# V as the moving operand in four column tiles, and shared weight loads for the scores, in a decode attention and MLP kernel

## The chip, the cores and the metric

The kernel runs on one core of a Trainium2 chip (trn2). The time is microseconds on the device. Before the change it is 372.0 us, the median of three runs (371.48 to 372.11).

## The reference

One token for each of 8 sequences goes through a gated mix of two branches: attention over a window of 2,048 cached positions, and an MLP.

```python
W = min(4096, max(256, Sk // 4))              # 2048
q = (x @ wq)                                  # 8 x 32 heads x 128
k = k_cache[:, :, Sk - W:, :]                 # 8 x 16 KV heads x 2048 x 128, bf16
v = v_cache[:, :, Sk - W:, :]                 # the same size; two query heads share a KV head
p = softmax(q k^T * Dh**-0.5)
a = (p v) @ wo                                # wo: 4096 x 576
b = gelu(layernorm(x) @ w1 + b1) @ w2 + b2    # w1: 576 x 4608, w2: 4608 x 576
out = g * a + (1 - g) * b                     # g = sigmoid(x . gate_w)
```

K and V of the window are 134 MB, the weights about 20 MB, and every byte is used for few rows only: one of K or V for the two query heads that share it, one of a weight for the 8 tokens. The kernel is a stream of loads.

## The kernel before

The sync engine issues one long list of loads. K and V come in "units" of 2 MB (four sequences of one head); 32 units each, in nine SBUF slots of 16 KB per partition. A group is four K units (all sequences of two heads). A planner orders every engine's work from estimated costs. The w2 chunks come last.

For a K unit, VectorE transposes K in place, then TensorE multiplies it by block-diagonal queries. Each 512-column matmul has its own weight load, although four in a row use the same one:

```python
for ee in range(2):
    for rc in range(4):
        rhs = bass.AP(arena, offset=aoffs("KT") + kb * 4096 + rc * 1024 + ee, ap=[[AST, 128], [2, 512]])
        mm = e.matmul(ps[:, rc, :], qbd[:, ub, 2 * h + ee, :], rhs, start=False, stop=(q == 3 and h == 1 and ee == 1))
```

For a V unit, V itself is the stationary operand, in 64 loads of 128x128, and eight probability columns move over each:

```python
for r in range(64):
    mm = e.matmul(ps[:, BK_OS[item % 2], 8 * (q % 2):8 * (q % 2) + 8], slot(s)[:, r * 128:(r + 1) * 128],
                  PT[:, g % 2, r, 8 * q:8 * q + 8],
                  start=(q % 2 == 0 and r == 0), stop=(r == 63), skip_group_check=True)
```

## Time and profile before

| what | before | where it is read |
|---|---|---|
| device time, median of 3 | 372.0 us | times |
| span of the profiled run | 369.5 us | page, first line |
| data queue, share of 16 engines' span | 98.5% | page, part 3 |
| TensorE, weight loads, VectorE, ScalarE busy | 65, 37, 57, 8% | page, part 1 |
| TensorE clock in the last four slices | 0.5 to 0.6 | page, part 2 |

In the profiles PE is TensorE's matmuls, PEld its weight loads, DVE VectorE, ACT ScalarE, POOL GpSimd and SP the sync engine; `ps` is PSUM, the memory that matmuls write, and `arena` the kernel's SBUF. These are the rows of the page's second part that matter (the span in 40 slices: granted TensorE clock in tenths, DMA busy in tenths, GB/s) and, from the third, the data queue and the queue of the instructions (packets, MB, share of 16 engines):

```profile
PEclk9999998799698879686898879696957788785556
DMA  8999999999999999999999999999999999999994
GB/s 343 426 422 424 427 432 431 434 424 431 429 431 429 413 436 427 429 427 429 435 426 429 414 431 432 431 431 426 426 435 433 418 424 427 435 429 426 413 420 167
...
q1 hardware_dynamic: 14848, 154.29, 98.5%
q8 instruction: 24, 0.39, 0.4%
```

DMA is at 9 tenths in every slice but the ends, and the data queue at 98.5%, so the loads bound the kernel. The instructions themselves are also read by DMA: the page has a queue of them, with 24 packets of 16 KB.

The groups of instructions by line (busy us, mean ns, then the idle time before them) for the weight loads of the scores and the products with V:

```profile
L641 PEld LDWEIGHTS ps<-arena 128*128 128x128 bf16 x512 | 52.5, 109 | 129.2 <-DVE arena L627 53.2 <-issue 39.2
L663 PE MATMUL ps<-arena 128*128 128x8 bf16 x2048 | 56.4, 166 | 12.3 <-DMA arena<-in_A_v_cache_dram 12.3
```

The timeline of TensorE at the end of the kernel before (start us, us, line, count, and the idle time before with what ended it):

```profile
357.10 2.33 PE L530 MATMUL ps<-arena 128*8 128x288 bf16 x18 [0.51 <-DMA arena<-in_B_w_dram]
360.06 2.33 PE L530 MATMUL ps<-arena 128*8 128x288 bf16 x18 [0.63 <-DMA arena<-in_B_w_dram]
363.15 3.96 PE L530 MATMUL ps<-arena 128*8 128x288 bf16 x36 [0.77 <-DMA arena<-in_B_w_dram]
...
367.25 0.45 DVE L734 CAST arena<-ps 8x288 bf16<-8x288 f32 x1 [14.28 <-PE ps L530]
```

The first three lines are w2 chunks 0, 1, and 2 with 3.

What the DMA engines do is in the windows view (start and end, length; busy us and counts of PE, PEld, DVE, ACT and POOL; then clock, DMA share and GB/s).

### The profile page before, as it was taken

What the parts mean: (1) busy time and instruction counts of PE and PEld (TensorE: products, weight loads), DVE (VectorE), ACT (ScalarE), POOL (GpSimd) and SP (SyncE); (2) the same over time, 40 slices, a digit from 0 to 9 for tenths busy, and PEclk for the clock granted to TensorE, in tenths of its full rate; (3) what the DMA queues carried; (4) which work ended last, traced back from release to release, by engine and by line L of the source; (5) the groups of instructions that cost most, each with busy time, mean ns of one, the idle gap of its engine ahead of it and who ended that gap; (6) DMA issues with size and microseconds to landing.
All of it is one profiled execution on the core that took longest, in us unless ns stands there. A gap on an engine that the chain in (4) does not pass through costs nothing.

```text
span 369.5 us, 7044 instructions
## 1 busy us (share of the span) xinstructions
PE 242.0 (65%) x3089; PEld 137.5 (37%) x3117; DVE 210.0 (57%) x253; ACT 28.6 (8%) x85; POOL 37.5 (10%) x163
## 2 busy tenths in 40 slices
PE   0349983896695486663965395755767385783376
PEld 0339430454242243232523243432424243343343
DVE  0704699688694663459744764478544964464000
ACT  1010001100300200003000300003000300003000
POOL 7030010011011001000101010100101000000000
PEclk9999998799698879686898879696957788785556
DMA  8999999999999999999999999999999999999994
GB/s 343 426 422 424 427 432 431 434 424 431 429 431 429 413 436 427 429 427 429 435 426 429 414 431 432 431 431 426 426 435 433 418 424 427 435 429 426 413 420 167
DMA packets 14934, 154.77 MB, mean 419 GB/s; under 512 B 1292, under 2 KB 5428, under 8 KB 6072
## 3 DMA queue, kind: packets, MB, share of 16 engines
q1 hardware_dynamic: 14848, 154.29, 98.5%
q8 instruction: 24, 0.39, 0.4%
q14 instruction: 6, 0.05, 0.0%
q10 hardware_dynamic: 56, 0.03, 0.0%
HBM read 154.31 MB, written 0.01 MB: 418 GB/s over the span
## 4 chain that ended last, share of the span: by engine, by line
DMA 63%; PE 20%; DVE 13%; SPq 2%; issue 1%; DVEq 0%
DMA arena<-in_A_k_cache_dram 42%; PE ps L641 12%; DMA arena<-in_B_w_dram 11%; DMA arena<-in_A_v_cache_dram 10%; DVE arena L627 9%; PE ps L663 3%; DVE arena L574 2%; PE ps L487 2%; SPq L716 1%; PE ps L530 1%; PE ps L637 1%; SPq L657 1%; PE ps L489 1%; DVE arena L577 0%; DVE arena L593 0%
## 5 line engine op out<-in xcount | busy, mean ns | idle before, releaser
L627 DVE STREAM_TRANSPOSE arena<-arena 128x2048 f32<-128x2048 f32 x64 | 145.0, 2296 | 79.1 <-DMA arena<-in_A_k_cache_dram 74.6
L641 PE MATMUL ps<-arena 128*128 128x512 bf16 x491 | 144.6, 449 | 45.1 <-DVE arena L627 44.0
L641 PEld LDWEIGHTS ps<-arena 128*128 128x128 bf16 x512 | 52.5, 109 | 129.2 <-DVE arena L627 53.2
L663 PE MATMUL ps<-arena 128*128 128x8 bf16 x2048 | 56.4, 166 | 12.3 <-DMA arena<-in_A_v_cache_dram 12.3
L663 PEld LDWEIGHTS ps<-arena 128*128 128x128 bf16 x2048 | 56.1, 97 | 19.1 <-DMA arena<-in_A_v_cache_dram 14.2
L620 POOL COPY arena<-arena 32x32 bf16<-32x32 bf16 x128 | 26.0, 203 | 177.2 <-PE ps L641 162.6
L637 PE MATMUL ps<-arena 128*128 128x512 bf16 x25 | 12.3, 630 | 40.2 <-DVE arena L593 36.7
L588 ACT ACTIVATE arena<-ps,arena 128x512 bf16<-128x512 f32 x32 | 21.5, 685 | 107.4 <-DVE arena L583 107.4
L574 DVE TENSOR_REDUCE arena<-ps 128x1 f32<-128x2048 f32 x8 | 18.3, 2282 | 17.7 <-PE ps L641 17.7
L593 DVE STREAM_TRANSPOSE arena<-arena 128x512 bf16<-128x512 bf16 x32 | 19.9, 675 | 0.9 <-ACT arena L588 0.9
L637 PEld LDWEIGHTS ps<-arena 128*128 128x128 bf16 x32 | 3.5, 128 | 42.9 <-DVE arena L593 38.5
L530 PE MATMUL ps<-arena 128*8 128x288 bf16 (+1 forms) x140 | 14.7, 377 | 3.1 <-DMA arena<-in_B_w_dram 1.9
L685 POOL TENSOR_TENSOR arena<-arena 128x16 bf16<-128x16 f32 x15 | 4.0, 265 | 121.2 <-ACT arena L678 121.2
L678 ACT ACTIVATE arena<-ps 128x16 f32<-128x16 f32 x15 | 2.8, 184 | 170.2 <-PE ps L663 170.2
L487 PE MATMUL ps<-arena 128*128 128x8 bf16 x144 | 10.9, 201 | 4.6 <-DMA arena<-in_B_w_dram 4.6
L487 PEld LDWEIGHTS ps<-arena 128*128 128x128 bf16 x144 | 10.8, 160 | 5.0 <-DMA arena<-in_B_w_dram 5.0
L530 PEld LDWEIGHTS ps<-arena 128*8 128x8 bf16 (+1 forms) x140 | 7.1, 106 | 10.9 <-DMA arena<-in_B_w_dram 3.6
L599 DVE RECIPROCAL arena<-ps 128x32 f32<-128x32 f32 x8 | 2.9, 358 | 11.4 <-PE ps L598 11.4
L409 PE MATMUL ps<-arena 8*128 8x8 bf16 x8 | 0.5, 167 | 13.4 <-DVE arena L382 9.7
L734 DVE CAST arena<-ps 8x288 bf16<-8x288 f32 x1 | 0.4, 446 | 14.3 <-PE ps L530 14.3
L685 DVE TENSOR_TENSOR arena<-ps,arena 128x16 bf16<-128x16 f32 x1 | 0.2, 228 | 14.0 <-PE ps L663 14.0
L489 PE MATMUL ps<-arena 128*128 128x8 bf16 x36 | 7.2, 201 | 0.0
(79 smaller groups left out, 79.4 us busy)
## 6 DMA issues: line engine op xcount, KB each, us to landing
arena<-in_A_k_cache_dram SPq DMA_DIRECT2D x32, 2048.0 KB, 34.0
arena<-in_A_v_cache_dram SPq DMA_DIRECT2D x32, 2048.0 KB, 34.4
arena<-in_B_w_dram SPq DMA_DIRECT2D x1, 4608.0 KB, 24.2
arena<-in_A_wo_dram SPq DMA_DIRECT2D x4, 1152.0 KB, 37.3
arena<-in_A_wq_dram SPq DMA_DIRECT2D x1, 4096.0 KB, 13.0
arena<-in_B_w_dram SPq DMA_DIRECT2D x3, 1296.0 KB, 14.8
arena<-in_B_w_dram SPq DMA_DIRECT2D x2, 576.0 KB, 20.5
arena<-in_A_wq_dram SPq DMA_DIRECT2D x1, 512.0 KB, 3.6
```

Source lines behind the costliest of these rows:

```text
L487: ins = e.matmul(out_, lhsT, yT[:, kt, :], start=(kt == 0), stop=False)
L489: ins = e.matmul(out_, lhsT, yT[:, 4 + c // 2, :], start=False, stop=True)
L530: ins = e.matmul(ps[32 * j:32 * j + 8, BK_ACC, 0:JN], lhsT, rhs[:, JN * j:JN * j + JN], start=False, stop=True, skip_group_check=True, til ...
L574: mx = add("dve", lambda e: e.tensor_reduce(out=k(MX), in_=ps[:, 0:4, :].rearrange("p a n -> p (a n)"), axis=AXL.X, op=ALU.max), deps=[qk_ ...
L588: return e.activation(out=Pm[:, 512 * c:512 * c + 512], in_=ps[:, c, :], func=ACTF.Exp, bias=k(NB), scale=SCALE, accum_out=k(SUM + c))
L593: pts.append(add("dve", (lambda c=c: lambda e: e.transpose(PT[:, g % 2, 16 * c:16 * c + 16, :].rearrange("p r m -> p (r m)"), Pm[:, 512 * ...
L620: return e.tensor_copy(dst, src)
L627: tr = add("dve", (lambda h=h, kb=kb: lambda e: e.transpose(bass.AP(arena_f, offset=foffs("KT") + kb * 2048, ap=[[AST // 2, 128], [1, 2048]]),
L637: mm = e.matmul(ps[:, rc, :], maskL, maskR, start=True, stop=False)
L641: mm = e.matmul(ps[:, rc, :], qbd[:, ub, 2 * h + ee, :], rhs, start=False, stop=(q == 3 and h == 1 and ee == 1))
L663: mm = e.matmul(ps[:, BK_OS[item % 2], 8 * (q % 2):8 * (q % 2) + 8], slot(s)[:, r * 128:(r + 1) * 128], PT[:, g % 2, r, 8 * q:8 * q + 8], ...
L685: return e.tensor_tensor(out=oT[:, item, :, :].rearrange("p h b -> p b h"), in0=src_.rearrange("p (b h) -> p b h", h=2), in1=rg[:, g % 2, ...
```

## The change

It is meant to relieve TensorE. V moves, 512 columns at a time, past 32 probability columns (four positions of eight). Four such matmuls go to four column tiles of 32 columns, so 16 matmuls take the place of 64 loads and 64 small matmuls. Of each 32x512 product only the diagonal blocks are wanted; ScalarE copies the product to SBUF, and four float32 matmuls with pieces of an identity pick the diagonal. The score matmuls that share a stationary matrix load it once (the page has 512 weight loads for them before). The core of the diff:

```diff
+def held_matmul(nc, e, out, lhsT, rhs, start=False, stop=True, skip=False, ...):
+    # a matmul instruction with ldweights=False: it uses the weights that are loaded
...
-                        for rc in range(4):
-                            mm = e.matmul(ps[:, rc, :], maskL, maskR, start=True, stop=False)
+                        e.matmul(ps[:, 0, :], maskL, maskR, start=True, stop=False)
+                        for rc in range(1, 4):
+                            held_matmul(nc, e, ps[:, rc, :], maskL, maskR, start=True, stop=False)
...
-                            mm = e.matmul(ps[:, rc, :], qbd[:, ub, 2 * h + ee, :], rhs, start=False, stop=(...))
+                            mm = e.matmul(*args, start=False, stop=last) if rc == 0 else held_matmul(nc, e, *args, stop=last)
...
-                for r in range(64):
-                    mm = e.matmul(ps[:, BK_OS[item % 2], 8 * (q % 2):8 * (q % 2) + 8], slot(s)[:, r * 128:(r + 1) * 128], PT[:, g % 2, r, 8 * q:8 * q + 8], ...)
+                for t in range(16):
+                    c = 32 * (t % 4)
+                    mm = e.matmul(ps[c:c + 32, BK_OS[i % 2], :], PT[:, g % 2, 512 * q + 32 * t:512 * q + 32 * t + 32], slot(s)[:, 512 * t:512 * t + 512],
+                                  start=(t < 4), stop=(t >= 12), skip_group_check=True, tile_position=(0, c))
...
+            u_ev[i] = add("act", lambda e: e.activation(out=EV[:, i % 2, :], in_=ps[:, BK_OS[i % 2], :], func=ACTF.Copy), ...)
+            def us_fn(e):
+                for r in range(4):
+                    mm = e.matmul(ps[:, BK_S, ...], EV[:, i % 2, 128 * r:128 * r + 128], i32[:, 8 * r:8 * r + 8],
+                                  start=(r == 0), stop=(r == 3), skip_group_check=True)
```

The rest (cut) is the layout of the transposed probabilities, the buffers, and the dependencies of PSUM bank 6, which now holds the selected sums too. The loads, their order and their slots are unchanged.

More of the change, by code (lines that the diff above doesn't have):

```diff
@@ L169, with held_matmul @@
 ARENA_BASE = 16512
+def held_matmul(nc, e, out, lhsT, rhs, start=False, stop=True, skip=False, tile_size=(128, 128), tile_position=(0, 0)):
+    return e.add_instruction(mybir.InstMatmult(
+        name=nc.get_next_instruction_name(), engine=mybir.EngineType.PE,
+        ins=[e.lower_ap(rhs), e.lower_ap(lhsT)], outs=[e.lower_ap(out)],
+        start_tensor_calc=start, stop_tensor_calc=stop, is_transpose=False, bass_skip_group_check=skip,
+        tile_size=tile_size, tile_position=tile_position, ldweights=False))
 def build_kernel(nc, A_x, A_k_cache, A_v_cache, A_wq, A_wo, B_x, B_w1, B_b1, B_w2, B_b2, gate_w, out):
@@ L244, in build_kernel @@
         req("o32", 2 * 16, F32)
+        req("EV", 2 * 512, F32)
         req("oT", Hkv * 16, BF)
@@ L305, in build_kernel @@
         out_sb = view("out_sb")
-        PT = view("PT").rearrange("p (g r m) -> p g r m", g=2, m=32)
+        PT = view("PT").rearrange("p (g n) -> p g n", g=2)
         Pm = view("P")
+        EV = view("EV").rearrange("p (u n) -> p u n", u=2)
         RAW = view("RAW")
@@ L334, in build_kernel @@
         BK_ACC = 7
+        OC = 64
         eng_sems = {e: es.enter_context(nc.semaphore("sem_" + e)) for e in ENGS}
@@ L558, in build_kernel @@
         o_item_ev = {}
+        u_ev, u_sum = {}, {}
+        b6_w, b6_r = [], [o_yT, o_gb]
         proj_ops = {}
@@ L592, in softmax @@
             for c in range(4):
-                pts.append(add("dve", (lambda c=c: lambda e: e.transpose(PT[:, g % 2, 16 * c:16 * c + 16, :].rearrange("p r m -> p (r m)"), Pm[:, 512 * c:512 * c + 512]))(),
+                pts.append(add("dve", (lambda c=c: lambda e: e.transpose(bass.AP(arena, offset=aoffs("PT") + 2048 * (g % 2) + 128 * c, ap=[[AST, 128], [8, 16], [512, 4], [1, 8]]), Pm[:, 512 * c:512 * c + 512].rearrange("p (r q m) -> p r q m", q=4, m=8)))(),
                                deps=[exs[c]] + ([pv_last[g - 2]] if g >= 2 else [o_yTp, o_b1p]), name="pt%d_%d" % (g, c), cost=0.62, prio=5))
@@ L597, in softmax @@
             ds = add("dve", lambda e: e.tensor_scalar(out=dsum, in0=i32, scalar1=k(S), scalar2=None, op0=ALU.mult), deps=[s_] + o_i32 + ([rg_done[g - 1]] if g else []), name="ds_%d" % g, cost=0.16, prio=5)
-            sp_ = add("pe", lambda e: e.matmul(ps[:, BK_S, 0:32], ones_f, dsum, start=True, stop=True), deps=[ds, o_yT, o_gb], name="sum_pe%d" % g, cost=0.5, prio=5)
+            sp_ = add("pe", lambda e: e.matmul(ps[:, BK_S, 0:32], ones_f, dsum, start=True, stop=True), deps=[ds] + b6_r[-2:], after=b6_w[-1:], name="sum_pe%d" % g, cost=0.5, prio=5)
+            b6_w.append(sp_)
             rc = add("dve", lambda e: e.reciprocal(out=rr, in_=ps[:, BK_S, 0:32]), deps=[sp_], name="rc_%d" % g, cost=0.16, prio=5)
+            b6_r.append(rc)
             def rg_fn(e):
@@ L640, in qk_fn @@
                             rhs = bass.AP(arena, offset=aoffs("KT") + kb * 4096 + rc * 1024 + ee, ap=[[AST, 128], [2, 512]])
-                            mm = e.matmul(ps[:, rc, :], qbd[:, ub, 2 * h + ee, :], rhs, start=False, stop=(q == 3 and h == 1 and ee == 1))
+                            args = (ps[:, rc, :], qbd[:, ub, 2 * h + ee, :], rhs)
+                            last = q == 3 and h == 1 and ee == 1
+                            mm = e.matmul(*args, start=False, stop=last) if rc == 0 else held_matmul(nc, e, *args, stop=last)
                     return mm
@@ L661, in pv_fn @@
                 mm = None
-                for r in range(64):
-                    mm = e.matmul(ps[:, BK_OS[item % 2], 8 * (q % 2):8 * (q % 2) + 8], slot(s)[:, r * 128:(r + 1) * 128], PT[:, g % 2, r, 8 * q:8 * q + 8],
-                                  start=(q % 2 == 0 and r == 0), stop=(r == 63), skip_group_check=True)
-                return mm
-            deps = [d] + pt_done[g]
-            if q % 2 == 0:
-                deps += [o_item_ev[item - 2]] if item >= 2 else [o_qT, o_u]
-            prev = add("pe", pv_fn, deps=deps, name="pv%d" % i, cost=2.2, after=pv_hist[-1:])
+                for t in range(16):
+                    c = 32 * (t % 4)
+                    mm = e.matmul(ps[c:c + 32, BK_OS[i % 2], :], PT[:, g % 2, 512 * q + 32 * t:512 * q + 32 * t + 32], slot(s)[:, 512 * t:512 * t + 512],
+                                  start=(t < 4), stop=(t >= 12), skip_group_check=True, tile_position=(0, c))
+                return mm
+            deps = [d] + pt_done[g] + ([u_ev[i - 2]] if i >= 2 else [o_qT, o_u])
+            prev = add("pe", pv_fn, deps=deps, name="pv%d" % i, cost=1.5, after=pv_hist[-1:])
             pv_hist.append(prev)
@@ L673, in v_unit @@
                 pv_last[g] = prev
+            u_ev[i] = add("act", lambda e: e.activation(out=EV[:, i % 2, :], in_=ps[:, BK_OS[i % 2], :], func=ACTF.Copy),
+                          deps=[prev] + ([u_sum[i - 2]] if i >= 2 else []), name="uev%d" % i, cost=0.8, prio=3)
+            def us_fn(e):
+                mm = None
+                for r in range(4):
+                    mm = e.matmul(ps[:, BK_S, OC + 16 * (item % 2) + 8 * (q % 2):OC + 16 * (item % 2) + 8 * (q % 2) + 8], EV[:, i % 2, 128 * r:128 * r + 128], i32[:, 8 * r:8 * r + 8],
+                                  start=(r == 0), stop=(r == 3), skip_group_check=True)
+                return mm
+            u_sum[i] = add("pe", us_fn, deps=[u_ev[i]] + o_i32 + b6_r[-2:], after=b6_w[-1:], name="us%d" % i, cost=1.0, prio=3)
+            b6_w.append(u_sum[i])
             if q % 2 == 1:
-                bk = BK_OS[item % 2]
                 hl = q // 2
+                prev = u_sum[i]
+                osrc = ps[:, BK_S, OC + 16 * (item % 2):OC + 16 * (item % 2) + 16]
                 if item < Hkv - 1:
-                    ev = add("act", lambda e: e.activation(out=o32[:, item % 2, :], in_=ps[:, bk, 0:16], func=ACTF.Copy), deps=[prev] + ([oT_done[item - 2]] if item >= 2 else []), name="oev%d" % item, cost=0.25, prio=3)
+                    ev = add("act", lambda e: e.activation(out=o32[:, item % 2, :], in_=osrc, func=ACTF.Copy), deps=[prev] + ([oT_done[item - 2]] if item >= 2 else []), name="oev%d" % item, cost=0.25, prio=3)
                     o_item_ev[item] = ev
+                    b6_r.append(ev)
                     eng, src_, deps = "pool", o32[:, item % 2, :], [ev, rg_done[g]]
                 else:
-                    eng, src_, deps = "dve", ps[:, bk, 0:16], [prev, rg_done[g]]
+                    eng, src_, deps = "dve", osrc, [prev, rg_done[g]]
                 def om_fn(e):
```

## The prediction

> **What bounds the kernel now.** The loads. The page moves 154.8 MB in a span of 369.5 us; its row of 40 slices has DMA at 9 of 10 everywhere but the first and last, at 413 to 436 GB/s, and the data queue takes 98.5% of the 16 engines' span. [...] 4 us windows show no dependence on compute: 426 GB/s with PE idle (248-252 us), 434 with PE full (100-104 us). 154.3 MB at about 428 GB/s is 361 us, plus 2 us to start and a tail: last weights land at 363.1 us, 36 projection matmuls (3.98 us), an evacuation (0.45), the store.
> The chain of waits names DVE (13%) and PE (20%), but loads take 34 us from issue to landing, about seven 2 MB transfers of 4.9 us ahead, so those waits do not empty the queue.
>
> **What the change does, per K and V unit pair (9.8 us of DMA).**
> - V products: 64 V weight loads with 8 moving columns (1.58 us at full clock, 1.87 at half) become 16 matmuls of 512 columns in four column tiles. Score matmuls of 512 columns come every 0.219 us at full clock. Column tiles overlap in this trace: 16 projection matmuls of 288 columns in two tiles took 1.10 us (0.07 each) where 288/512 of 0.219 is 0.12. Estimate: four rounds, 0.9 us, 1.8 at half clock; without overlap 3.5 or 7.
> - Shared loads: 408 fewer of about 109 ns, 44 us of PEld busy. But score matmuls stream (8 in 1.75 us) with loads hidden.
> - Added ACT copy 128x512 from PSUM, like the exponential's 0.69 us: 22 us in all (ACT 8% to 14%).
> - Added four float32 selection matmuls; the float32 sum matmul takes two loads and two passes, 0.3-0.4 us, so about 1.5 us per unit.
> - Probability transposes write pieces of eight; 675 ns should stay.
> PE per pair: 3.5 + 0.9 + 1.5 = about 6 us at full clock, against 5.1; below 9.8. At half clock it nears 10[...].
>
> **On the critical path.** Almost nothing. About 2,900 fewer instructions (7,044 to some 4,100) halve the instruction queue's 0.4% DMA share: an estimated 0.7 us. In the tail, the last V unit's copy and selection add 2-3 us before its projection, absorbed because PE waits for w2 until 363 us anyway. Another clock in the final 36 matmuls moves it by up to 1.5 us.
>
> **Prediction: 371.3 us, 8 in 10 between 369.7 and 373.0.** Faster by over 2%: 0.02. Within 2%: 0.95. Slower: 0.03.
>
> **What would show it.** Data queue near 98.5%, slices still 413-436 GB/s, last w2 landing at 362-363.5 us. 16 V matmuls of a unit in 0.9-1.9 us. Score PEld down to a quarter while 8 score matmuls still take 1.75 us. ACT up 22 us. Instruction queue about 0.2 MB.
>
> **What would make it wrong.** If column tiles do not overlap, or selection matmuls stall PE in order behind ACT, V buffers come free late, the queue runs dry, load slices drop below 410: slower by 2% or more. Faster by 2% needs a DMA rate above 436 GB/s, which nothing here moves.

The forecast's sum: 372.0 us before, less the estimated 0.7 us for instruction packets, gives its 371.3. Over stretches of 40 us from 40 to 320 us the mean clock was 0.79 to 0.91 in before and 0.80 to 0.91 in after, where the data queue is at 98.9%.

## More of the kernel before

At the end come the w2 chunks. Each has 9 weight rows per partition, 18 matmuls of 288 columns (two column tiles). The last chunk is loaded in three pieces, so that little work is left after the last byte:

```python
cuts = [0, 4, 7, 9] if ci == FC - 1 else [0, FJ]
# ... one load per piece, then
mms = [(hT[:, FJ * ci + j, :], dst[:, j * D:(j + 1) * D]) for j in range(j0, j1)]
ops.append(AccGroup("m2_%d_%d" % (ci, n), mms, [o_hT, d], ...).op)
```

The kernel before, last microseconds:

```profile
360.00:362.00 2.00, 1.94 (x18) 1.02 (x18) 0.00 (x0) 0.00 (x0) 0.00 (x0) 0.50 0.95 396
362.00:363.00 1.00, 0.38 (x4) 0.00 (x0) 0.00 (x0) 0.00 (x0) 0.00 (x0) 0.50 0.58 239
363.00:364.00 1.00, 0.85 (x8) 0.49 (x10) 0.00 (x0) 0.00 (x0) 0.00 (x0) 0.50 0.53 219
364.00:365.00 1.00, 1.00 (x12) 0.53 (x8) 0.00 (x0) 0.00 (x0) 0.00 (x0) 0.50 0.53 215
365.00:366.00 1.00, 1.00 (x12) 0.54 (x10) 0.00 (x0) 0.00 (x0) 0.00 (x0) 0.50 0.38 146
```

From 362 us on the DMA share is 0.58, then 0.53 for two microseconds: half of the 16 engines are done, and the other half need four microseconds more.

## The result, and the profile after

The changed kernel is correct and took 369.38 us (median of 4, 369.3 to 369.6) against 371.74 us before (4 runs). The ratio is 0.9937, 95% interval 0.9923 to 0.9951: about 2.4 us faster, below the range's low end of 369.7, and within 2%. A ratio is the mean time of one kernel's runs over that of the other's of the same rounds, so it is not quite the ratio of the medians. Executions over 1.5% slower than the fastest of the same kernel are left out of the means. Run again later it was 369.50 us beside 371.39, ratio 0.9944.

The same rows of the page of the kernel after:

```profile
PEclk9999999699599869887897869886996879886659
DMA  8999999999999999999999999999999999999994
GB/s 345 428 412 424 435 430 433 428 428 428 433 429 431 422 433 426 428 435 427 433 431 433 408 434 432 429 426 433 433 436 428 414 434 424 431 433 440 402 429 193
...
q1 hardware_dynamic: 14848, 154.29, 98.9%
...
q8 instruction: 13, 0.21, 0.2%
```

The middle is as full of loads as before. There are 13 instruction packets instead of 24, for 4,129 instructions instead of 7,044. The groups that answer to those of before:

```profile
L659 PEld LDWEIGHTS ps<-arena 128*128 128x128 bf16 x128 | 15.0, 117 | 124.6 <-issue 71.3 <-DVE arena L642 53.3
L682 PE MATMUL ps<-arena 128*32 128x512 bf16 x512 | 36.4, 410 | 2.9 <-DMA arena<-in_A_v_cache_dram 2.9
L697 PE MATMUL ps<-arena 128*128 128x8 f32 x256 | 35.3, 269 | 8.7 <-ACT arena L691 7.7 <-DVE arena L613 1.0
L691 ACT ACTIVATE arena<-ps 128x512 f32<-128x512 f32 x32 | 19.1, 598 | 196.8 <-PE ps L682 196.8
```

The operations cost about what had been estimated, the selection matmuls less (35.3 us in 32 units, 1.1 each, against 1.5). TensorE even became busier (72% of the span, 65% before), which is why the difference must be looked for elsewhere. The end of TensorE's timeline after:

```profile
361.93 2.01 PE L541 MATMUL ps<-arena 128*8 128x288 bf16 x26 [1.82 <-DMA arena<-in_B_w_dram]
...
364.34 0.54 PE L541 MATMUL ps<-arena 128*8 128x288 bf16 x6 [0.41 <-DMA arena<-in_B_w_dram]
...
365.06 0.41 PE L541 MATMUL ps<-arena 128*8 128x288 bf16 x4 [0.18 <-DMA arena<-in_B_w_dram]
...
365.61 0.45 DVE L764 CAST arena<-ps 8x288 bf16<-8x288 f32 x1 [11.14 <-PE ps L541]
```

Now TensorE waits for each piece, and the last wait is the true last landing. Chunk 2 is ready 1.2 us earlier (361.93, before 363.15), and TensorE's wait for the last piece ends 0.3 us after its landing at 364.72 us (below); its work ends 0.4 us later, at 365.47. The windows of the kernel after:

```profile
360.00:362.00 2.00, 0.17 (x4) 0.08 (x4) 0.00 (x0) 0.00 (x0) 0.00 (x0) 1.00 0.94 383
362.00:363.00 1.00, 1.00 (x18) 0.65 (x18) 0.00 (x0) 0.00 (x0) 0.00 (x0) 1.00 0.66 257
363.00:364.00 1.00, 0.85 (x12) 0.27 (x8) 0.00 (x0) 0.00 (x0) 0.00 (x0) 1.00 0.38 141
364.00:365.00 1.00, 0.54 (x6) 0.18 (x6) 0.00 (x0) 0.00 (x0) 0.00 (x0) 1.00 0.13 48
365.00:366.00 1.00, 0.41 (x4) 0.09 (x4) 0.39 (x1) 0.40 (x1) 0.00 (x0) 1.00 0.00 0
```

Two differences: the clock is 1.0 instead of 0.5, and the late engines leave one after another instead of all together, earlier. The first engines finish at about 362 us in both.

In the packet records of the trace, the last data packet ends 365.96 us after the start of the span before, 364.72 after. I call this the last landing below. The records also show the durations of the 16 KB instruction packets, in ns. Before:

```
879 936 938 922 964 962 954 881 | 878 935 938 928 962 962 949 879 | 879 934 931 924 961 968 947 893
```

The pattern repeats every eight packets. That, and the half of the engines that ends late, suggested a theory.

**Theory F (fetch, slowest engine).** TensorE's instruction packets go round eight of the 16 DMA engines. Each load of a unit or of w2 sends 16 semaphore increments, and a unit is 128 packets of 16 KB; I take both as an even cut over 16 engines, so an engine that also reads instructions falls behind. A load has landed only when its last increment is in (after: the last increment at 365.02 us, TensorE starts on that piece at 365.06). The end is set by the fullest engine: three packets before (24 / 8), two after (13 / 8, rounded up). The packet records do not name the engine: which packets share one is read from their times, from the DMA share and from the increments.

**Theory S (fetch, spread).** The packets cost their share of all 16 engines: the prediction's form.

**Theory C (clock of the tail).** The float32 selection matmuls keep TensorE busy near the end, so that the w2 projections run at full clock.

F and C can both be true. The experiments separate them.

### The profile page after: what moved, and what is told of

It reads as the page before. It is cut to its first block, busy times and chain, and to the rows that moved or that the text cites. A ratio compares the mean times of both kernels' runs of the same rounds, so it can differ in the third digit from the quotient of the medians.

```text
span 367.9 us, 4129 instructions
## 1 busy us (share of the span) xinstructions
PE 263.5 (72%) x1837; PEld 87.0 (24%) x1429; DVE 210.4 (57%) x253; ACT 47.8 (13%) x117; POOL 37.5 (10%) x163
## 3 DMA queue, kind: packets, MB, share of 16 engines
q1 hardware_dynamic: 14848, 154.29, 98.9%
## 4 chain that ended last, share of the span: by engine, by line
DMA 61%; PE 20%; DVE 16%; SPq 1%; issue 1%; ACT 0%; DVEq 0%; ACTq 0%
DMA arena<-in_A_k_cache_dram 50%; DMA arena<-in_B_w_dram 11%; DVE arena L642 10%; PE ps L173 9%; PE ps L659 3%; DVE arena L587 3%; PE ps L498 2%; PE ps L682 2%; PE ps L697 2%; DVE arena L606 1%; DVE arena L590 1%; PE ps L500 1%; SPq L675 1%; DVE arena L596 0%; SPq L746 0%
## 5 line engine op out<-in xcount | busy, mean ns | idle before, releaser
L173 PE MATMUL ps<-arena 128*128 128x512 bf16 x408 | 141.3, 462 | 0.0
L659 PE MATMUL ps<-arena 128*128 128x512 bf16 x128 | 58.8, 459 | 21.4 <-DVE arena L642 21.3
L691 ACT ACTIVATE arena<-ps 128x512 f32<-128x512 f32 x32 | 19.1, 598 | 196.8 <-PE ps L682 196.8
L659 PEld LDWEIGHTS ps<-arena 128*128 128x128 bf16 x128 | 15.0, 117 | 124.6 <-issue 71.3
L697 PE MATMUL ps<-arena 128*128 128x8 f32 x256 | 35.3, 269 | 8.7 <-ACT arena L691 7.7
L697 PEld LDWEIGHTS ps<-arena 128*128 128x128 f32 x256 | 34.0, 208 | 21.8 <-ACT arena L691 15.2
L682 PE MATMUL ps<-arena 128*32 128x512 bf16 x512 | 36.4, 410 | 2.9 <-DMA arena<-in_A_v_cache_dram 2.9
L651 PE MATMUL ps<-arena 128*128 128x512 bf16 x8 | 4.7, 585 | 40.8 <-DVE arena L606 40.8
L682 PEld LDWEIGHTS ps<-arena 128*32 128x32 bf16 x512 | 11.3, 100 | 37.4 <-issue 27.1
L498 PE MATMUL ps<-arena 128*128 128x8 bf16 x144 | 10.9, 201 | 4.7 <-DMA arena<-in_B_w_dram 4.7
L541 PE MATMUL ps<-arena 128*8 128x288 bf16 (+1 forms) x140 | 11.9, 316 | 2.9 <-DMA arena<-in_B_w_dram 2.8
L498 PEld LDWEIGHTS ps<-arena 128*128 128x128 bf16 x144 | 10.8, 157 | 5.2 <-DMA arena<-in_B_w_dram 5.2
L651 PEld LDWEIGHTS ps<-arena 128*128 128x128 bf16 x8 | 0.9, 107 | 45.1 <-DVE arena L606 45.1
```

The source lines that it names most:

```text
L173: return e.add_instruction(mybir.InstMatmult(name=nc.get_next_instruction_name(), engine=mybir.EngineType.PE, ins=[e.lower_ap(rhs), e.lowe ...
L498: ins = e.matmul(out_, lhsT, yT[:, kt, :], start=(kt == 0), stop=False)
L541: ins = e.matmul(ps[32 * j:32 * j + 8, BK_ACC, 0:JN], lhsT, rhs[:, JN * j:JN * j + JN], start=False, stop=True, skip_group_check=True, til ...
L659: mm = e.matmul(*args, start=False, stop=last) if rc == 0 else held_matmul(nc, e, *args, stop=last)
L682: mm = e.matmul(ps[c:c + 32, BK_OS[i % 2], :], PT[:, g % 2, 512 * q + 32 * t:512 * q + 32 * t + 32], slot(s)[:, 512 * t:512 * t + 512], st ...
L691: u_ev[i] = add("act", lambda e: e.activation(out=EV[:, i % 2, :], in_=ps[:, BK_OS[i % 2], :], func=ACTF.Copy), deps=[prev] + ([u_sum[i - ...
```

## The experiments

Twelve runs were made: eleven new kernels, and the kernel after again. All were correct. They fell on several chips, so each is compared with before. "Landing" is the last landing. The right column is DMA share times 16 shortly before the landing (windows below), where it was looked at.

| kernel | time, us | of before | packets | landing, us | engines left |
|---|---|---|---|---|---|
| before (profile) | 371.39 to 371.76 | | 24 | 365.96 | 8.0 |
| after (profile; run again) | 369.38; 369.50 | 371.74; 371.39 | 13 | 364.72; 364.43 | 5.4 |
| b_warm | 370.98 | 371.55 | 25, the last at 365.9 us | 365.93 | |
| b_held | 371.69 | 371.55 | 23 | 365.89 | 6.9 |
| b_pad | 374.60 | 371.55 | 35 | 369.12 | 3.0 |
| a_pad | 374.82 | 371.55 | 24 | 365.98 | |
| a_pad16 | 369.65 | 371.53 | 16 | 364.37 | 7.8 |
| a_pad18 | 370.85 | 371.53 | 18 | 365.84 | 2.1 |
| a_noheld | 369.46 | 371.39 | 14 | 364.45 | 6.4 |
| a_cold | 370.27 | 371.53 | 13 | 364.44 | |
| a_k8 | 372.69 | 371.53 | 13 | 365.62 | |
| a_pool | 398.91 | 371.39 | 13 | 382.57 | |
| a_pool2 | 371.49 | 371.76 | 13 | 366.83 | 1.1 |

### b_warm: the clock alone

```diff
+        def warm(n, chain, deps=()):      # n matmuls of zeros into the PSUM bank that is free by then
+            ... e.matmul(ps[:, BK_S, 0:512], zeros_bf, maskR, start=True, stop=True, skip_group_check=True)
...
+            if i in (29, 30, 31):
+                warm({29: 10, 30: 10, 31: 8}[i], pv_hist)
...
+            if ci < 2:
+                warm(4, o_m2)             # after w2 chunks 0 and 1
```

> The kernel before, with 36 idle 128x512 matmuls of zero weights put on PE between the last V units and w2 chunks, into the PSUM bank that nothing uses any more; about 72 instructions more, nothing else. Theory C (clock of the tail): part of the gain came from PE running the final w2 projection at full instead of half clock, because the selection matmuls kept it busy there. C expects the granted clock at 1.0 when the last 36 projection matmuls run, these 2.2 us or less instead of 3.98, PE's end about 0.45 us behind the last landing instead of about 1.3, and 0.7 to 1.0 us off the time. Theory F (instruction fetch: fewer PE instruction packets let the slowest DMA engines end earlier) expects the last landing where it was (within 0.3 us) and, if it were alone, no gain.

370.98 us against 371.55, ratio 0.9984 (0.9972 to 0.9996). The landing did not move (365.93). The timeline of b_warm's tail:

```profile
363.21 2.04 PE L530 MATMUL ps<-arena 128*8 128x288 bf16 x26 [0.86 <-DMA arena<-in_B_w_dram]
...
366.43 0.41 PE L530 MATMUL ps<-arena 128*8 128x288 bf16 x4 [0.23 <-DMA arena<-in_B_w_dram]
```

Chunk 2 starts as late as before (363.21), but now TensorE catches up and waits for the last piece. So C is real, and worth 0.57 us alone (0.15 to 1.04 by the interval), a little below the 0.7 to 1.0 expected. TensorE ends 0.91 us behind the landing, 1.15 in the profile of before; I had expected 0.45. C is not the whole. (The 25th instruction packet starts at 365.9 us, with the landing, and so does not move it.)

### a_pad: TensorE's instruction count restored

```diff
             def us_fn(e):
                 mm = None
+                for _ in range(52 if i < 28 else 0):
+                    e.matmul(ps[:, BK_S, 256:264], zeros_bf, maskR[:, 0:8], start=True, stop=True, skip_group_check=True)
```

> The kernel after, with 52 extra pairs of a weight load and an 8-column matmul of zeros ahead of each of the first 28 selection groups: 2,912 instructions more, so that PE reads as many as before (about 24 packets of 16 KB), the tail untouched. Theory F in its form of the slowest engine: before, the instruction packets come in a pattern of durations that repeats every 8, so they seem to go round 8 of the 16 DMA engines, three packets of 0.93 us on each; after, two on the fullest. F expects the last landing about 0.9 us later and the time up by 0.8 to 1.1 us. If the cost is spread over all 16 engines (my prediction's form) it is 11 x 0.93 / 16 = 0.65 us. Theory C expects no change while the tail's clock stays full.

The landing went back to 365.98, that of before. But the time rose to 374.82 us: the padding took 1.5 us per V unit, TensorE fell behind, and in the profile its last 92 w2 and wo matmuls begin only at 362.4 us and run 8.3 us without a wait. One of six runs (392.6) is left out. The landing speaks for F; the time is spoilt by my padding.

### b_pad: more instructions on the kernel before

```diff
+                for _ in range(100 if q % 2 == 0 and i < 28 else 0):
+                    e.matmul(ps[:, BK_OS[item % 2], 256:264], zeros_bf, maskR[:, 0:8], start=True, stop=True, skip_group_check=True)
                 for r in range(64):
```

> The kernel before with 100 extra pairs of a weight load and an 8-column matmul of zeros ahead of every second V unit up to the 28th: 2,800 instructions more, about 35 instruction packets instead of 24. F in the form of the slowest engine: five packets on the fullest of 8 engines instead of three, last landing 1.9 us later, time up by 1.6 to 2.2 us. Spread over 16 engines: 11 x 0.93 / 16 = 0.65 us. C: no change.

374.60 us, 3.05 up; landing 3.16 us later. S (0.65) is excluded. F's direction and order are right, its size is not: the two extra packets cost 1.6 us each rather than 0.93. Part of that may not be F: the loads slowed in slices near 350 us, and the eight early engines ended at about 363.6 instead of 362. The last 36 projections took 4.48 us at half clock, 3.96 in the profile of before.

### b_held: the shared weight loads alone

The diff is the part of the change that brings held_matmul into the score and mask matmuls, put on the kernel before.

> The kernel before with the shared weight loads of the score and mask matmuls alone (408 fewer weight loads). All theories: score matmuls still 8 in 1.75 us at full clock. F: 22 or 23 instruction packets instead of 24, still three on the fullest engine, so the last landing and the time within 0.3 us of before. C: the tail is not touched, no change.

371.69 us against 371.55, ratio 1.0007 (0.9994 to 1.0020). It does nothing, as expected: the loads were hidden behind the 512-column matmuls, which at full clock start 0.226 us apart with a load each (profile of before, from 45.5 us) and 0.225 us apart where four share one (after, from 302.3 us).

### a_noheld: the V part alone

The kernel after, with ordinary matmuls for scores and masks.

> The kernel after without the shared weight loads: 408 weight loads put back, V in column tiles kept. 14 or 15 instruction packets, at most two on each of the 8 engines. F in the slowest-engine form: last landing at 364.4 to 364.8, time within 0.4 us of after, so that the shared loads give nothing and all of the gain is of the V products' side. Against it would be a loss of 1 us or more.

369.46 us, as after on the same chip (369.50). All of the gain comes with the V products. They, and not the shared loads, carry both the fewer instructions and the busier tail.

### a_pad16 and a_pad18: across the step from two packets to three

The padding of a_pad, with 14 and with 24 pairs per unit.

> The kernel after with 14 extra pairs of a weight load and an 8-column matmul ahead of each of the first 28 selection groups: 784 instructions, 15 or 16 instruction packets of 16 KB in place of 12 or 13, at most two on each of 8 DMA engines, as after. The slowest-engine form of F: last landing at 364.7 us as after, time within 0.4 us of after. The spread form: 3 x 1.2 / 16 = 0.2 us later. C: no change while the tail's clock stays full.

> The same with 24 pairs: 1,344 instructions, about 18 packets, 17 of them before the end, so one or two engines get a third. The slowest-engine form of F: last landing one whole packet later than after, 1.2 us by the runs so far (the first padded kernel landed 1.26 us later than after), time up by 0.9 to 1.3 us over after. The spread form: 5 x 1.2 / 16 = 0.4 us. PE has less padding than in the first padded kernel, whose PE ran 8 us late into the tail, so its end should not set the time here.

With 16 packets: 369.65 us, landing 364.37, as after. Four runs lie at 369.4 to 369.7 and two at 370.4 and 370.6. The profile fell on one of the latter, and there TensorE is at 0.5 until 363.7 us and, late from the padding too, never waits for the last pieces: this fits C, but does not show it alone. With 18 packets: 370.85 us, landing 365.84, 1.47 us later for two packets more. Three packets more (13 to 16) cost nothing, the next two cost all. This is the step of F, and S cannot make it.

The windows show it directly. One line each, just before the last landing, of before, after, b_held, a_noheld, a_pad16, a_pad18 and b_pad in this order; the second number from the right is the DMA share:

```profile
364.70:365.40 0.70, 0.70 (x10) 0.40 (x6) 0.00 (x0) 0.00 (x0) 0.00 (x0) 0.50 0.50 201
```
```profile
363.50:364.20 0.70, 0.43 (x8) 0.09 (x2) 0.00 (x0) 0.00 (x0) 0.00 (x0) 1.00 0.34 123
```
```profile
364.70:365.40 0.70, 0.70 (x10) 0.38 (x8) 0.00 (x0) 0.00 (x0) 0.00 (x0) 0.50 0.43 158
```
```profile
363.30:363.80 0.50, 0.47 (x8) 0.12 (x4) 0.00 (x0) 0.00 (x0) 0.00 (x0) 1.00 0.40 159
```
```profile
363.20:363.90 0.70, 0.70 (x12) 0.36 (x8) 0.00 (x0) 0.00 (x0) 0.00 (x0) 0.60 0.49 194
```
```profile
364.70:365.40 0.70, 0.47 (x8) 0.12 (x4) 0.00 (x0) 0.00 (x0) 0.00 (x0) 1.00 0.13 51
```
```profile
367.20:368.20 1.00, 1.00 (x12) 0.51 (x8) 0.00 (x0) 0.00 (x0) 0.00 (x0) 0.50 0.19 77
```

Times 16, the engines still busy are 8.0, 5.4, 6.9, 6.4, 7.8, 2.1 and 3.0. The packets are 24, 13, 23, 14, 16, 18 and 35; over eight engines, those holding one more than the rest (or all of them, if it divides) number 8, 5, 7, 6, 8, 2 and 3. No other theory here gives these counts.

The trace also records each semaphore increment, and needs no choice of a window. The last load gets 16, as many as there are engines. In before eight come by 363.95 us and eight between 365.96 and 366.30; in a_pad18 eight by 364.00, six from 364.54 to 364.90 and two at 366.23 and 366.25; in b_pad eight by 364.03, five from 367.40 to 367.67 and three from 368.98 to 369.42. In before the time between a unit's first and last increment is about 1.8 us up to the ninth instruction packet (139.4 us), 3.0 after it, and 4.4 after the 17th (262.4 us), with smaller steps between: the large ones come where a new round of eight begins. That also answers a rival, that padding keeps TensorE from freeing buffers in time and so delays the loads: in a_pad18 that would have moved more than two increments.

### a_cold: the clock taken away from after

```diff
+                if ci < 2:      # the first two w2 chunks wait for three tiny GpSimd writes, which wait for the matmuls before
+                    for w in range(3):
+                        gap = [add("pool", lambda e: e.memset(dg, 0.0), deps=gap, ...)]
```

> The kernel after with two short pauses on PE, before the first and before the second w2 chunk, each a wait for three tiny GpSimd writes, some 0.7 us, as long as the gaps that the kernel before has there. At full clock they cost nothing, since the last two chunks land at 362 us and later. C: the clock stays at 0.5 in the tail in most runs, the last 36 projection matmuls take some 4 us again, and the time rises by 0.6 to 2.0 us with the last landing unchanged at 364.7. F alone: no change.

370.27 us, in two clusters: 369.26, 369.59, 369.76 and 370.78, 371.00, 371.02. The landing is 364.44 as expected. The profiled run, of the upper cluster, has chunk 0 at half clock (2.32 us for 18 matmuls) and TensorE 2.3 us behind the landing. If the half clock makes the upper cluster, as this one profile has it, the tail's clock is worth up to 1.4 us when the landing is early, and the short pauses took it away in three of six runs; I had expected most. The pauses also delay TensorE (0.64 and 0.63 us idle in that profile), so the size is an upper bound.

### a_k8: the last piece in loads of 8 rows

```diff
+                if ci == FC - 1 and j1 == FJ:     # the last piece: 16 loads of 8 rows instead of one of 128
+                    for p in range(0, 120, 8):
+                        d = dma("sp", ... e.dma_start(dst[p:p + 8, j0 * D:j1 * D], src[p:p + 8, j0 * D:j1 * D]) ...)
```

> The kernel after with its last w2 piece (288 KB, 128 rows of 2,304 bytes) split in 16 loads of 8 rows. [...] F says the 16 engines end unevenly: eight near 362 us, the others up to 2.7 us later. If the eight are those without instruction packets, the fullest engines carry 18 KB less: last landing 0.6 to 0.7 us earlier, time 0.5 us down. If they are the ones with the packets, the last landing is 0.6 to 0.8 us later. If all engines ended together (F wrong), 36 KB on half the engines costs 0.7 us.

The cut sentence said how many and which of the 16 engines serve a load of 8 rows; no run had shown it then. "The eight" are the engines of such a load. Its trace has eight increments for each of these loads where the others have 16.

372.69 us. The last data packet ended at 365.62 us, 0.9 or 1.2 us later than in the two profiles of after. That is near what was expected if the eight engines of these loads are the eight that also read TensorE's instructions, but the semaphore records speak against it: the first increment of these loads comes at 361.32 us, 0.24 us after the first of the piece before, so early engines have a share in them. Which engines they are is not shown, nor whether loads of 8 rows are slower by themselves. On top, TensorE's wait ended only at 367.78 us, 2.2 us after the last data packet, where it is 0.3 to 0.5 us in after and b_warm. In the trace the 16 loads send 128 increments, eight each, and the last five arrive 0.2 us apart, until 367.74; the 16 of after's last piece are in by 365.02. Why they trail the data is open. In this form, relieving the late engines makes it worse.

### a_pool and a_pool2: instructions of another engine

```diff
+                    for n in range(66 * i, 66 * i + 66 if a == 0 else 0):     # a_pool2: 40 a unit, from the ninth unit on
+                        e.memset(view("scr")[32 * (n % 4):32 * (n % 4) + 8, n // 4:n // 4 + 1], 0.0)
```

> The kernel after with 2,112 one-element writes on GpSimd, 66 ahead of each K unit's query copies, into memory that nobody reads: some 8 more instruction packets, for an idle engine, PE as after. If every engine's instructions are fetched by the same 8 DMA engines, each gets one packet more: last landing and time 1.0 to 1.4 us later. If GpSimd's are fetched by the other 8, which end 2.7 us earlier, no change in the last landing (within 0.3 us). If instruction bytes mattered only for TensorE's own waiting, no change either, but then the eight early DMA engines would still end at 362.

398.91 us, inconclusive: the writes take 95 ns each, 199.7 us in all, GpSimd could not prepare the queries in time, and that held up the loads (29.4 us over after run again). Its packets came on the other instruction queue, in 8 KB pieces, and the last 3 us had one engine busy alone. Hence the lighter second one:

> The kernel after with 960 one-element writes on GpSimd, 40 ahead of the query copies of each K unit from the ninth on: 3.8 us of GpSimd per unit pair of 9.8 us at the 95 ns that the first such kernel showed, so that GpSimd, which stopped the loads there, does not bound this one. The first one's extra instruction packets came as 8 KB ones on the other instruction queue, some 16 for 2,112 instructions, and its last 3 us had one DMA engine busy alone. So here some 7 or 8 more 8 KB packets. If they all go to one engine and it is among the eight late ones, the last landing is 2 us or more later with one engine busy alone at the end; if it is among the eight early ones, their 2.7 us of slack hide it and nothing changes; if they are spread, no change beyond 0.4 us.

371.49 us, 2.0 above after run again (on another chip; the ratio to before is 1.0000, that of after 0.9944); landing 366.83, 2.4 us later than on the second run of after. The instruction queues and the last window of a_pool2:

```profile
q8 instruction: 13, 0.21, 0.2%
...
q14 instruction: 14, 0.11, 0.1%
```
```profile
365.30:366.60 1.30, 0.76 (x10) 0.37 (x12) 0.00 (x0) 0.00 (x0) 0.00 (x0) 1.00 0.07 27
```

Eight packets more than after on the second queue (14, after 6), and 0.07 x 16 = one engine left alone. I read this as one DMA engine for all of these GpSimd instructions; 64 KB of them cost the whole kernel 2 us. By the increments it is not one of the eight that read TensorE's: the time between the first and the last of a load's 16 increments grows from 1.9 us (load landing at 131 us) to 5.2 (at 352), by 0.5 to 0.6 with each of the six extra packets in between, and by nothing with TensorE's. Eight of those come from 142 us on, by F one for each of the eight engines. So it should be an early engine. I had expected its 2.7 us of slack to hide the eight extra packets; at 0.55 us each they make 4.4.

## Why the prediction was wrong

Right:
- The bound. Loads fill the middle before and after (data queue 98.5 and 98.9%), and the middle slices are alike.
- The costs of the parts. 16 V matmuls of a unit took 1.05 us at full clock and 1.90 at half (predicted 0.9 to 1.9), so the column tiles overlap: one after another, at the 0.226 us between score matmuls in the trace of before (0.219 in the prediction), 16 would take 3.6 us. The score weight loads fell from 52.5 to 15.0 us. The probability transposes stayed at 674 ns. ScalarE rose by 19 us (22 predicted). The instruction queue moved 0.21 MB (0.2 predicted).
- The shared loads give nothing: b_held 1.0007.

Wrong:
- The failed step: "About 2,900 fewer instructions (7,044 to some 4,100) halve the instruction queue's 0.4% DMA share: an estimated 0.7 us." The mechanism was right, the size was not, since 0.2% was taken of all 16 engines. By the counts above the packets sit on eight of them and the fullest counts. Each also costs more than the 0.93 us that the share counts (below). a_pad18 (three packets, full clock) against after run again (two packets, full clock) is 370.85 - 369.50 = 1.35 us; the landings of before and after differ by 1.24.
- The term left out: "Another clock in the final 36 matmuls moves it by up to 1.5 us." I gave it no sign. The float32 selection matmuls of the last V unit (352.3 to 354.2 us) and the 38 projection matmuls behind them leave TensorE without gaps until 358.4 us, and the clock rises at 357.7. b_warm puts it at 0.57 us on the kernel before. The trace of before shows a dense stretch that starts at half clock (TensorE is busy throughout 96 to 100 us at 0.50, and at 0.98 from 100 to 104), and it has the clock at 0.5 from 332 to 366 us, with gaps of 0.5 to 0.8 us between bursts of 2.3 in the last 9 us of that. I did not apply this to the tail.
- A misread line: "last weights land at 363.1 us". That was chunk 2. The last landing was 365.96 and hidden behind a TensorE at half clock, so both terms above were invisible to me in the chain of waits.

The sum closes within the noise. In the two profiles the landing comes 1.24 us earlier and TensorE's end 0.40 us closer behind it (0.75 us, before 1.15), together 1.64, and the spans differ by 1.6. By the runs it is 1.35 + 0.57 = 1.92 us against 371.39 - 369.50 = 1.89, but the 1.35 compares two chips; each against before, a_pad18 and after differ by 1.21. The 2.36 of the first comparison is no contradiction: its interval is 1.8 to 2.9 us, and the runs of before alone spread from 370.8 to 372.9.

Why a 16 KB packet of 0.93 us sets its engine back by 1.2 to 1.6 us can be read from the packet records of before: with each such packet between 73 and 347 us, one engine's data stop for 0.86 to 0.95 us, and its next 16 KB data packet takes 1.07 to 1.16 us where nearly all others take 0.61. Together that is an estimated 1.4 us. Three of these after 361.8 us, where the early engines end (the last load's first increment comes at 361.70 us before and 361.87 after), give 366.0 (landing 365.96), two give 364.6 (364.72), five 368.8 (b_pad, 369.12).

No kernel here was clearly faster than after. The next step of F would need at most eight packets. At the 250 instructions a packet that 3,266 TensorE instructions in 13 packets make, that is an estimated 2,000, which no small edit reaches.

## What to carry to other kernels

When a kernel is bound by loads, look at the last microseconds by DMA engine. Here the DMA share fell to one half and stayed there (0.53 from 363 to 365 us in before): some engines carried extra work, and the end was set by the fullest, not by the average (landing 364.37 us with 16 packets, 365.84 with 18). Instructions were such work here, those of GpSimd too (a_pool2: eight more packets of 8 KB, landing 2.4 us later). So a form with fewer instructions paid although its compute lies off the critical path, in steps of one packet on the fullest engine. Whether another kernel has the same, its own packet records must show. And a last wait in the timeline was not the last landing while the waiting engine was slow (363.15 against 365.96 us in before): check where the data packets end.
